# A DeltaNet recurrence and a SwiGLU feed-forward block: chunks of 64 tokens on 64x64 array tiles, with the triangular inverse moved from TensorE to VectorE

## The chip, the cores and the metric

The kernel runs on one core of one Trainium2 chip. The metric is the device time of the whole program in microseconds, as the median of a kernel's runs. Every kernel was run beside the kernel before on the same chip.

## The reference, cut to what matters

```python
# q, k, v: (4, 8, 768, 48) float32; beta: (4, 8, 768)
k_n = k / (np.linalg.norm(k, axis=-1, keepdims=True) + 1e-06)
for t in range(S):                                   # 768 tokens, one after the other
    kt, vt, bt = (k_n[:, :, t], v[:, :, t], beta[:, :, t, None])
    y[:, :, t] = np.einsum('bhd,bhde->bhe', q[:, :, t], state)
    v_old = np.einsum('bhde,bhd->bhe', state, kt)
    state = state + bt[:, :, :, None] * np.einsum('bhd,bhe->bhde', kt, vt - v_old)
# ... y becomes x: (4*768 tokens, 384)
g = x @ w_gate                                       # 384 x 1536
val = x @ w_val                                      # 384 x 1536
out = (g * (1.0 / (1.0 + np.exp(-g))) * val) @ w_out # 1536 x 384
```

The three weights arrive as float64, and the kernel has to turn them into fp32 itself.

## The kernel before

The tokens of one batch element are cut into chunks of C = 128. With S the state before a chunk and A, P the strictly lower triangles of two products of the chunk's rows, U = (I + A)^-1 (V - K S), Y = Q S + P U, and S grows by W^T U. A *unit* is one batch element and one chunk: 24 units. The inverse is built on TensorE by doubling: blocks of 2, 4, ... 128 rows, each level joined by two products and one transpose per head.

```python
        for s in levels:                             # 2, 4, 8, 16, 32
            p_a = ps_att([128, H, HC], "p_a")
            for h in range(H):
                nc.tensor.matmul(
                    p_a[:, h].rearrange("p (n r) -> p n r", r=s),
                    gq[:, h, 0],
                    even(x[:, h], s),
                )
            ax = work.tile([128, H, HC], FP32, name="ax")
            # ... VectorE: ax = p_a * sibling[s]
            yield
            p_d = ps_att([128, H, HC], "p_d")
            for h in range(H):
                nc.tensor.matmul(p_d[:, h], xt[:, h], ax[:, h])
            # ... VectorE: even blocks of x -= p_d
            yield
            transpose(xt, x)                         # 8 transposes (p_x) and 2 copies on ScalarE
            yield
        # ... the last level on halves of the rows; then U, Y, the new state, Y^T

    def ffn(c):                                      # a chunk of all four batch elements: 512 tokens
        for f in range(FT):
            # gate and val: KT = 3 matmuls each of 128 weight columns by 512 tokens
            # sil = Silu(p_gate) on ScalarE, h_f = sil * p_val on VectorE
        for b in range(B):
            # p_o: FT = 12 matmuls of 384 columns
    # emission: steps of two units in flight, steps of the FFN of an earlier chunk among them
```

Before the first FFN, VectorE converts the weights in 60 pieces with seven instructions each, one piece per round of the recurrence's steps.

## Time and profile before

| | before |
|---|---|
| time, median of 3 runs first, 4 runs beside the changed kernel | 1638.46 us, 1637.99 us |
| span of the profiled run | 1633.6 us |
| TensorE busy; records | 1519.6 us (93%); 9102 |
| VectorE, ScalarE, GpSimd busy | 30%, 17%, 15% |
| mean granted TensorE clock | 0.909 |

The profile counts every fp32 matmul as two records. "Busy" of TensorE is the time in which any record runs, so records of several array tiles that run side by side count once.

From the profile's page of the kernel before, the busy tenths of TensorE and VectorE in 40 equal slices (41 us each) and the granted clock in tenths; then the chain that ended last, by line:

```profile
PE   3985997999899999899899899899989999999999
...
DVE  7768764222122121222221212322122212122110
...
PEclk8875877999897799899899988789989989989999
...
PE p_a L347 15%; PE p_d L362 13%; PE p_gate L468 11%; PE p_val L468 10%; PE p_o L486 9%; PE p_x L325 8%; PE p_y L418 3%; POOL xt L328 3%; POOL xt L334 3%; PE p_u L400 3%; DVE gq L307 2%; DMA kpad<-in_k_dram 2%; PE p_d L384 2%; PE p_s L435 2%; POOL norm L267 1%
```

TensorE is nearly full from the third slice on. p_a, p_d and p_x, the three products of the inverse, are 15 + 13 + 8 + 2 = 38% of the chain, more than the whole FFN (11 + 10 + 9 = 30%). VectorE has room after the first six slices, where it converts weights.

### The profile page before, as it was taken

What the parts mean: (1) busy time and instruction counts of PE and PEld (TensorE: products, weight loads), DVE (VectorE), ACT (ScalarE), POOL (GpSimd) and SP (SyncE); (2) the same over time, 40 slices, a digit from 0 to 9 for tenths busy, and PEclk for the clock granted to TensorE, in tenths of its full rate; (3) what the DMA queues carried; (4) which work ended last, traced back from release to release, by engine and by line L of the source; (5) the groups of instructions that cost most, each with busy time, mean ns of one, the idle gap of its engine ahead of it and who ended that gap; (6) DMA issues with size and microseconds to landing.
All of it is one profiled execution on the core that took longest, in us unless ns stands there. A gap on an engine that the chain in (4) does not pass through costs nothing.

```text
span 1633.6 us, 21195 instructions
## 1 busy us (share of the span) xinstructions
PE 1519.6 (93%) x9102; PEld 1184.1 (72%) x9102; DVE 486.5 (30%) x1070; ACT 281.5 (17%) x531; POOL 247.2 (15%) x186
## 2 busy tenths in 40 slices
PE   3985997999899999899899899899989999999999
PEld 2984975776796777688577689577769767768745
DVE  7768764222122121222221212322122212122110
ACT  1121221111121121112112112112111212211210
POOL 6004016003103100401300500500120210020000
PEclk8875877999897799899899988789989989989999
DMA  8322201001001000101000100100100000000000
GB/s 182 91 75 52 59 11 29 1 10 26 10 16 20 1 1 11 29 11 28 2 1 11 30 10 11 20 1 1 25 10 11 15 1 1 6 11 10 1 0 20
DMA packets 90238, 35.09 MB, mean 21 GB/s; under 512 B 79360, under 2 KB 83968, under 8 KB 90144
## 3 DMA queue, kind: packets, MB, share of 16 engines
q1 hardware_dynamic: 86688, 29.01, 8.5%
q10 hardware_dynamic: 3456, 4.72, 0.8%
q8 instruction: 72, 1.18, 0.3%
q14 instruction: 22, 0.18, 0.0%
HBM read 29.00 MB, written 4.72 MB: 21 GB/s over the span
## 4 chain that ended last, share of the span: by engine, by line
PE 81%; POOL 10%; DVE 5%; DMA 2%; issue 1%; ACT 0%; POOLq 0%; SPq 0%
PE p_a L347 15%; PE p_d L362 13%; PE p_gate L468 11%; PE p_val L468 10%; PE p_o L486 9%; PE p_x L325 8%; PE p_y L418 3%; POOL xt L328 3%; POOL xt L334 3%; PE p_u L400 3%; DVE gq L307 2%; DMA kpad<-in_k_dram 2%; PE p_d L384 2%; PE p_s L435 2%; POOL norm L267 1%
## 5 line engine op out<-in xcount | busy, mean ns | idle before, releaser
L347 PEld LDWEIGHTS p_a<-x,gq 128*128 128x128 f32 x1920 | 261.0, 220 | 12.2 <-issue 9.6
L347 PE MATMUL p_a<-x,gq 128*128 128x64 f32 x1920 | 259.8, 301 | 0.0
L362 PEld LDWEIGHTS p_d<-ax,xt 128*128 128x128 f32 x1920 | 229.0, 197 | 13.4 <-issue 10.7
L362 PE MATMUL p_d<-ax,xt 128*128 128x64 f32 x1920 | 229.7, 280 | 0.0
L468 PE MATMUL p_gate<-x_ffn,wg_sb 128*128 128x512 f32 x432 | 212.6, 630 | 1.3 <-ACT x_ffn L458 1.1
L486 PE MATMUL p_o<-wo_sb,h_f 128*128 128x384 f32 x576 | 204.7, 504 | 0.0
L468 PE MATMUL p_val<-x_ffn,wv_sb 128*128 128x512 f32 x432 | 201.2, 602 | 0.0
L326 ACT COPY xt<-p_x 128x512 f32<-128x512 f32 x240 | 124.0, 595 | 419.8 <-PE p_x L325 419.8
L353 DVE TENSOR_TENSOR ax<-p_a,sibling 128x512 f32<-128x512 f32 x120 | 83.0, 691 | 370.2 <-PE p_a L347 369.8
L486 PEld LDWEIGHTS p_o<-wo_sb,h_f 128*128 128x128 f32 x576 | 109.1, 197 | 69.0 <-issue 10.6
L278 POOL TENSOR_TENSOR w<-kn,beta_t 128x512 f32<-128x512 f32 x24 | 25.4, 1058 | 782.2 <-PE p_s L435 781.8
L468 PEld LDWEIGHTS p_gate<-x_ffn,wg_sb 128*128 128x128 f32 x432 | 82.0, 202 | 84.1 <-issue 81.4
L364 DVE TENSOR_TENSOR x<-x,p_d 128x512 f32<-128x512 f32 x120 | 82.6, 688 | 192.6 <-PE p_d L362 192.6
L468 PEld LDWEIGHTS p_val<-x_ffn,wv_sb 128*128 128x128 f32 x432 | 78.4, 192 | 80.0 <-issue 79.7
L325 PEld LDWEIGHTS p_x<-ident,x 128*128 128x128 f32 x960 | 110.7, 146 | 17.6 <-issue 12.5
L325 PE MATMUL p_x<-ident,x 128*128 128x128 f32 x960 | 121.1, 279 | 0.0
L480 DVE TENSOR_TENSOR h_f<-sil,p_val 128x512 f32<-128x512 f32 x72 | 49.3, 685 | 237.1 <-PE p_val L468 237.0
L325 PE MATMUL p_x<-ident,xt 128*128 128x128 f32 x192 | 39.1, 370 | 76.0 <-POOL xt L334 76.0
L477 ACT ACTIVATE sil<-p_gate 128x512 f32<-128x512 f32 x72 | 43.0, 597 | 371.3 <-PE p_gate L468 371.3
L325 PEld LDWEIGHTS p_x<-ident,xt 128*128 128x128 f32 x192 | 31.0, 191 | 88.1 <-POOL xt L334 88.1
L328 POOL TENSOR_TENSOR xt<-gq,couple 128x1024 f32<-128x1024 f32 x24 | 56.9, 2372 | 165.3 <-DVE gq L307 165.3
L307 DVE SCALAR_TENSOR_TENSOR gq<-p_g,beta_t,mask_u 128x256 f32<-128x256 f32 x192 | 78.0, 474 | 12.8 <-PE p_g L304 12.8
(76 smaller groups left out, 1182.5 us busy)
## 6 DMA issues: line engine op xcount, KB each, us to landing
kpad<-in_k_dram SPq DMA_DIRECT2D x25, 192.0 KB, 4.4
qpad<-in_q_dram SPq DMA_DIRECT2D x25, 192.0 KB, 3.9
v_in<-in_v_dram SPq DMA_DIRECT2D x25, 192.0 KB, 2.8
staged<-in_moe_w_gate_dram SPq DMA_DIRECT2D x18, 256.0 KB, 3.7
staged<-in_moe_w_val_dram SPq DMA_DIRECT2D x18, 256.0 KB, 3.8
out_dram<-o_sb ACTq DMA_DIRECT2D x24, 192.0 KB, 1.9
staged<-in_moe_w_out_dram SPq DMA_DIRECT2D x12, 256.0 KB, 2.7
staged<-in_moe_w_out_dram SPq DMA_DIRECT2D x12, 128.0 KB, 2.0
```

The lines of the kernel that those rows point to most:

```text
L307: nc.vector.scalar_tensor_tensor(out=gq[:, h], in0=p_g[:, j], scalar=beta_t[:, c, b * H + h : b * H + h + 1], in1=mask_u[:, None, :].to_br ...
L325: nc.tensor.transpose(p_x[:, h], src[:, g + h], ident)
L326: nc.scalar.copy(dst[:, g : g + 4], p_x)
L328: nc.gpsimd.tensor_tensor(out=xt, in0=gq[:, :, 0], in1=couple[:, None, :].to_broadcast([128, H, 128]), op=ALU.mult,)
L334: nc.gpsimd.tensor_tensor(out=xt, in0=xt, in1=ident[:, None, :].to_broadcast([128, H, 128]), op=ALU.add,)
L347: nc.tensor.matmul(p_a[:, h].rearrange("p (n r) -> p n r", r=s), gq[:, h, 0], even(x[:, h], s),)
L353: nc.vector.tensor_tensor(out=ax, in0=p_a, in1=sibling[s][:, None, :].to_broadcast([128, H, HC]), op=ALU.mult,)
L362: nc.tensor.matmul(p_d[:, h], xt[:, h], ax[:, h])
L364: nc.vector.tensor_tensor(out=x_even, in0=x_even, in1=p_d.rearrange("p h j -> p (h j)").rearrange("p (n r) -> p n r", r=s), op=ALU.subtract,)
L468: nc.tensor.matmul(ps[name], w_sb[:, t, f * 128 : (f + 1) * 128], x[:, t], start=(t == 0), stop=(t == KT - 1),)
L480: nc.vector.tensor_tensor(out=h_f, in0=sil, in1=ps["p_val"], op=ALU.mult)
L486: nc.tensor.matmul(p_o, hs[f][:, b * C : (b + 1) * C], wo_sb[:, f], start=(f == 0), stop=(f == FT - 1),)
```

## The change

The intent is to take the inverse off TensorE, and to make the small products of the recurrence small on the array as well. Chunks become 64 tokens, so a unit is two batch elements of 64 tokens, and a head's product fits one 64x64 quarter of the array. Two chunks form a group: their 2 x 2 x 2 x 8 = 64 triangles of 64 rows give 128 diagonal blocks of 32x32, which go through DRAM so that each of VectorE's 128 partitions holds one block. There the inverse is made by substitution: 31 steps of a multiply and an add. It returns through DRAM, and two 32x32 products per head fill the off-diagonal block. The FFN runs per chunk of 256 tokens.

The core of the diff; "# ..." marks cuts:

```diff
-C = 128  # tokens of a chunk of the recurrence
+C = 64
+R = 32
# ... removed: masks of the levels, couple, the block mask of the state
-        for s in levels:
-            p_a = ps_att([128, H, HC], "p_a")
# ... removed: p_a, ax, p_d, x -= p_d, transposes p_x, per level; the last level
+    def prepare(g):
# ... norms and normalized k of two chunks, p_t: K^T and Q^T as before
+                p_g = ps_two([128, 2, NP, 2, C], "p_g")
+                for j in range(NP):
+                    for par, b in ((0, 0), (1, 1), (0, 1), (1, 0)):
+                        rows = slice(64 * par, 64 * par + 64)
+                        cols = slice(64 * b, 64 * b + 64)
+                        nc.tensor.matmul(
+                            p_g[cols, par, j],
+                            kq[n][rows, j, 0, cols],
+                            kq[n][rows, j, :, cols],
+                        )
# ... VectorE: a_sb and p_sb, masked
+        nc.sync.dma_start(out=a_d, in_=a_sb[g].rearrange("p u h i -> p (u h) i"))
# ... four reads of a_d into mb [128, 32, 32]: one block per partition
+        for j in range(R - 1):
+            m = R - 1 - j
# ...
+            nc.vector.tensor_tensor(
+                out=t_v,
+                in0=zb[:, 0 : j + 1, j : j + 1].to_broadcast([128, j + 1, m]),
+                in1=mb[:, j : j + 1, j + 1 : R].to_broadcast([128, j + 1, m]),
+                op=ALU.mult,
+            )
+            nc.vector.tensor_tensor(
+                out=zb[:, 0 : j + 1, j + 1 : R],
+                in0=zb[:, 0 : j + 1, j + 1 : R],
+                in1=t_v,
+                op=ALU.add,
+            )
# ... zb to z_d in DRAM, four reads into zt; then two 32x32 products (p_j) per head
+    ORDER = ((0, 0), (1, 1), (0, 1), (1, 0))
+    def advance(c):
# ... K S, Q S, U, the state and P U: 16 matmuls each, in this pattern
+                for j in range(NP):
+                    for par, b in ORDER:
+                        rows = slice(64 * b, 64 * b + 64)
+                        nc.tensor.matmul(
+                            p_s[64 * par : 64 * par + 64, b, j * D : (j + 1) * D],
+                            kn[rows, 2 * j + par],
+                            uu[rows, par, j],
# ...
     def ffn(c):
-        for f in range(FT):
+        for f in range(0, FT, 2):
# ... two weight blocks share a PSUM bank: [128, 2, 256]
+    some(prepare(0), everything)
+    some(advance(0), everything)
+    load_group(1)
+    behind = prepare(1)
+    some(behind, 10)
+    for c in range(NCH):
# ...
+        if c + 1 < NCH:
+            some(advance(c + 1), everything)
+        feed = ffn(c)
+        for n in range(FT // 2 + NB):
+            if c == 0:
+
+                some(converting, 2 * KT if n < FT // 2 else everything)
+            some(feed, 1)
+            some(behind, 2)
```

The order in which the program emits instructions is not quite the order on an engine: the build puts each engine's instructions in an order of its own that keeps to the dependences.

## The prediction

> **What bounds the kernel now.** I first read the busy shares on the page, then the share of the last chain by line, then the clock by stretch, and last the chain piece by piece to get the pace of each kind of matmul.
>
> ```profile
> PE 1519.6 (93%) x9102; PEld 1184.1 (72%) x9102; DVE 486.5 (30%) x1070; ACT 281.5 (17%) x531; POOL 247.2 (15%) x186
> ...
> PE 81%; POOL 10%; DVE 5%; DMA 2%; issue 1%; ACT 0%; POOLq 0%; SPq 0%
> ```
>
> TensorE is busy 93% and is 81% of the chain; nobody else is above 30%. So the question is how much TensorE time the change takes away, and whether waits then fill the space. A busy share says nothing about pace. That comes from the chain in order of time (start, length, line, records):
>
> ```profile
> 802.33 3.61 PE p_gate L468 x6
> 805.93 3.52 PE p_d L362 x32
> 809.45 2.63 PE p_val L468 x6
> 812.08 1.75 PE p_x L325 x16
> ...
> 816.41 3.52 PE p_a L347 x32
> ...
> 1599.41 30.97 PE p_o L486 x96
> ```
>
> Each fp32 matmul leaves two records (the code has 216 gate matmuls, the page 432; transposes leave one). The pace per record is 3.52/32 = 0.110 us for p_a and p_d (64 columns stream, 128 columns of weights), 1.75/16 = 0.109 for a transpose, 2.63/6 = 0.438 for 512 streamed columns (about 0.429 between steady starts), 30.97/96 = 0.323 for 384. The wide ones follow the streamed columns, 0.84 ns each; p_a and p_d do not, they follow the 128 weight columns. Two more lines, from the timeline of TensorE, show small array tiles:
>
> ```profile
> 917.68 2.10 PE L304 MATMUL p_g<-kq 64*128 64x256 f32 x16
> ...
> 1522.70 2.05 PE L384 MATMUL p_d<-xt,ax 64*64 64x64 f32 x32
> ```
>
> One tile of 64x64 alone steps at about (2.05-0.22)/31 = 0.059 us (0.22 is one record's length). The 64-row p_g, whose records alternate between the two row halves, steps at (2.10-0.38)/15 = 0.115, where 256 columns alone would cost 0.215: the two halves do run side by side.
>
> Full-clock sum: FFN 6 x (144 x 0.429 + 96 x 0.323) = 556 us. Recurrence: 3840 p_a/p_d x 0.110 = 422, 1152 p_x x 0.110 = 127, 768 p_u and p_y from u x 0.1125 = 86, 480 with the state x 0.1125 = 54, 384 p_g x 0.125 = 48, 264 other transposes x 0.11 = 29, 768 64x64 x 0.059 = 45: 811. Together 1367, and 1367/0.909 (mean granted clock) = 1504, against 1519.6 busy: the sum is sound.
>
> **What the Trainium skill says.** (1) "TensorE: Matmul & The Clock Gate", LDWEIGHTS: a weight load costs about P/1.2 ns, P its columns, whatever the rows: 107 ns for 128, 53 for 64. The trace agrees: 0.110 and 0.059. (2) "TensorEngine Tiling (Array Packing)", Key Properties: tiles work independently, weights and matmuls of different tiles in parallel, and a change of tiling mode drains the array. The trace shows two row tiles in parallel; four 64x64 tiles at once it does not show. (3) "VectorE: DVE Perf Modes", Mode 2x_2P: an fp32 tensor_tensor stays at one result a cycle. The trace agrees: 555 ns for 384 columns (L394), 691 for 512 (L353), so 1.06 ns a column plus about 150. (4) "DMA: Bandwidth & Descriptors", Anatomy of one DMA: about 2 us fixed (fitted there for the GpSimd path). The trace has 1.9 to 4.4 us to landing for 128 to 256 KB.
>
> **The change, part by part.** A unit is now two batches of 64 tokens; there are 24 again.
>
> *Removed:* all levels of p_a, p_d and p_x, 422+127+45 = 594 us of TensorE at full clock, with their copies on ACT (xt 124, x 27), DVE (ax 83, x 83) and POOL (xt 57+57).
>
> *Recurrence on small tiles, records per unit.* p_t 8 x 0.109 = 0.9 us. p_g 32 records, 128 streamed columns (0.107 alone), row halves alternating: two at once gives 0.054, 1.7 us. p_j 64 records of 32x32 on two row groups: estimate 0.025, 1.6. Advance: K S, Q S, U, state and P U are 16 matmuls each, 160 records, 64 weight columns and 48 streamed; 0.059 for a pair gives 0.03, 4.8. p_f 0.35. About 1.5 for changes of tile shape (my guess). Sum 10.9 us, 24 units = 260 us instead of 811.
>
> *FFN per 256 tokens.* 1728 records x 0.215 + 576 x 0.323 = 557 us: no change. Weight loads double, but 0.107 fits behind 0.215.
>
> So TensorE falls from 1367 to about 817 us at full clock.
>
> *Substitution, per group of two chunks (six groups).* 31 steps of two dependent DVE instructions; elements sum over j of (j+1)(31-j) = 5456, twice = 10912. RECIPROCAL after its input's instruction starts 35 ns after that one's end, so a dependent instruction costs about 150+35+1.04n: 62 x 0.185 + 10912 x 0.00104 = 11.5+11.3 = 23 us. Beside TensorE's 160 us per group this is small. Masks 8 x 0.62, norms 4, one multiply 1.1, transposes 1.4, copies 3: about 38 us of DVE per group.
>
> *Two round trips through DRAM per group.* 1 MB out (322 GB/s at best in this trace: 3.3 us, plus 2), then four reads of 1024 pieces; kpad, 1024 pieces too, takes 4.4 us to land and about 1.1 to issue: 4.4+3x1.1 = 7.7. About 13 us, and 11 for the way back. From the last mask to a usable zt, with the inverse's p_j: 13+23+11+10 = some 57 us of latency. Groups are prepared one to two chunks (46 us of FFN each) ahead, so in steady state most hides.
>
> **The start.** Here the change costs. Group 0 has nothing to hide behind: norms to about 13 us, four units at half clock to 35, then 57 or more and the advance: first FFN input near 115 to 130 us. And the weights' conversion is now emitted beside the first FFN chunk. By the page its DVE work is 155 us (L136 to L183 summed over both widths). DVE must do 155 + two groups x 38 + advances and h_f 8 = 239 us before that chunk is done, plus 15 of waits that conversion can't fill: about 254 us. TensorE runs perhaps 15 us ahead into chunk 1, so the rest starts as if at 240.
>
> **The rest, TensorE bound.** FFN 11 x 46.4 = 510. Prepare 16 units x 4.9 = 78; advance 20 units x 6 = 119 (drains shared out). Together 707 at full clock. The clock in the middle of the present run:
>
> ```profile
> 400.00:600.00 200.00, 188.33 (x1138) 151.71 (x1136) 46.23 (x81) 33.24 (x63) 32.60 (x20) 0.88 0.05 10
> 600.00:800.00 200.00, 187.66 (x1197) 146.76 (x1195) 48.61 (x90) 37.11 (x71) 41.22 (x28) 0.94 0.09 17
> 800.00:1000.00 200.00, 194.16 (x1203) 151.05 (x1203) 44.84 (x75) 33.94 (x65) 20.64 (x14) 0.96 0.05 11
> ```
>
> The eighth column is the clock. At 0.94, 707 becomes 752. Idle TensorE is 3 to 6% there; the new advance is a chain of short bursts, each waiting for a copy, and PSUM has two buffers where there were five, so I choose 10%: 835 us. 240+835 = 1075 us, a ratio of 0.66.
>
> **Rivals.** *No side-by-side tiles* (every 64x64 record 0.059): +4.6 advance, +1.7 p_g, +1 p_j per unit, about +150 us: 1225. For it: four tiles are not seen in the trace. Against: p_g shows two. *Round trips in the way:* if TensorE or the DVE's h_f stands behind each group's waiting instruction, up to 25 us for each of four groups, 1175. For it: engines take their instructions in order, and in the present trace TensorE stood 76 us for POOL's xt. Against: the conversion's instructions are interleaved across pieces on DVE, so the order is chosen with waits in mind. *DVE as the bound:* steady state needs 38 + 8 (h_f) + 6 of about 165 us per group, so no; at the start yes, and slower substitution steps or POOL in its way would add 30 to 60 us there. *Conversion done early*, in the idle start: 990 to 1010.
>
> **Range and chances.** The removed TensorE time is certain; pace of small tiles (+150), round trips (+100) and start (-60 to +60) are not, and the misses lean upward. I say 975 to 1220. Slower than 1606 would need 390 us of waits more than I count, after 140 allowed: 2%.
>
> **What would show it.** Right: TensorE busy near 900 us; advance records 0.03 us apart; gate and val 0.215; no L347, L362, L325 group; the first FFN chunk ending near 255 us with DVE full until then; clock at half before 100 us. Wrong: small-tile records 0.06 apart or more; TensorE below 80% after 260 us with DMA or DVE zb, mb as releaser; substitution above 30 us a group.

## The result, and the profile after

| | before | after |
|---|---|---|
| time, median of 4 runs each | 1637.99 us (1635.29 to 1639.12) | 952.32 us (951.05 to 954.01) |
| ratio | | 0.581, 95% interval 0.5795 to 0.5826 |
| TensorE busy; records | 1519.6 us; 9102 | 797.4 us; 8520 |
| VectorE busy | 486.5 us | 391.6 us |

A ratio is the mean time of one kernel's runs over the mean of the other's of the same rounds, so it is not quite the ratio of the medians. The result is 123 us below the prediction of 1075 and below its range.

From the page of the changed kernel: busy times, the same slices (24 us each now), and the chain by engine.

```profile
PE 797.4 (84%) x8520; PEld 609.6 (64%) x8520; DVE 391.6 (41%) x1079; ACT 132.7 (14%) x242; POOL 86.6 (9%) x84
...
PE   2400599466699998999989999989999999999998
...
DVE  4677228998823482222662122932124621101010
...
PE 65%; DVE 21%; DMA 5%; POOL 4%; issue 2%; SPq 1%; ACT 1%; ACTq 0%; POOLq 0%; DVEq 0%
```

There are two stages. For eleven slices, 262 us, TensorE has gaps (nine of the eleven tenths are 6 or less) and VectorE is often full; after that TensorE is full to the end. The end of the first FFN chunk (the copies of its two results start at 259.7 and 261.7 us) is the border. The rest, 689.9 us, is 72% of the span. The two stages in windows; the columns are the length, then busy time and instructions of TensorE, weight loads, VectorE, ScalarE and GpSimd, then the clock, the DMA share and GB/s:

```profile
60.00:90.00 30.00, 0.00 (x0) 0.00 (x0) 26.75 (x90) 0.00 (x0) 5.27 (x3) 1.00 0.06 25
90.00:120.00 30.00, 13.44 (x352) 12.03 (x352) 7.80 (x18) 3.37 (x9) 6.94 (x7) 1.00 0.22 39
...
160.00:200.00 40.00, 24.45 (x135) 16.86 (x133) 38.96 (x144) 1.79 (x3) 0.30 (x1) 0.74 0.26 76
200.00:260.00 60.00, 36.79 (x194) 21.43 (x194) 55.53 (x218) 2.58 (x6) 11.85 (x8) 0.91 0.42 111
```

```profile
262.00:400.00 138.00, 132.71 (x1709) 100.53 (x1712) 51.80 (x115) 24.16 (x48) 14.22 (x12) 0.98 0.21 46
400.00:600.00 200.00, 195.01 (x2158) 150.53 (x2149) 68.21 (x149) 33.31 (x59) 14.22 (x12) 0.99 0.22 48
600.00:800.00 200.00, 194.65 (x2260) 149.08 (x2260) 75.42 (x174) 32.74 (x64) 13.06 (x10) 0.98 0.14 31
800.00:950.00 150.00, 146.96 (x893) 114.97 (x892) 14.05 (x21) 17.23 (x32) 0.00 (x0) 1.00 0.03 8
```

In the start, VectorE alone works from 60 to 90 us (substitution of group 0 and some conversion), then idles, then is full from 160 us on with the rest of the conversion. In the rest, which I call the second stage, TensorE is busy 669.3 of 688 us, so idle 2.7%, at a clock of 0.98 to 1.00 (0.987 weighted by length).

Why is it so full? The timeline of TensorE in a piece of this stage (start, length, line, what, records):

```profile
319.74 2.10 PE L528 MATMUL p_o<-wo_sb,h_f 128*128 128x384 f32 x6
321.76 1.15 PE L428 MATMUL p_y<-state,kq 64*64 64x48 f32 x64
322.84 1.13 PE L511 MATMUL p_gate<-x_ffn,wg_sb 128*128 128x256 f32 x4
323.90 1.14 PE L447 MATMUL p_u<-r,zt 64*64 64x48 f32 x32
324.97 1.13 PE L511 MATMUL p_gate<-x_ffn,wg_sb 128*128 128x256 f32 x4
326.03 0.68 PE L463 MATMUL p_s<-uu,kn 64*64 64x48 f32 x32
326.53 1.10 PE L481 MATMUL p_y<-uu,p_sb 64*64 64x48 f32 x32
```

Three things are to be read here. The 64 records of K S and Q S step at (1.15 - 0.22)/63 = 0.015 us, 0.22 being one record's length. Between K S and U, and between U and the state, where a subtraction on VectorE or a copy on ScalarE must come first, stand four records of gate, about 1.1 us of other work: no idle time is noted. The program emits advance(c + 1) as a whole before ffn(c), so it is the build's order that put them there. And a change between 128x128 and 64x64 tiles is not free. On the way in, six p_o records should take 6 x 0.323 = 1.94 us from 319.74 to 321.68, and the small ones start at 321.76. Then four gate records should take 4 x 0.2155 = 0.86 us, and from 322.84 to 323.90 they take 1.06. Decoded from the trace, in the second stage: the last gate or val record before a small burst takes 0.309 us instead of 0.216, the first one after it 0.320, and the last small record mostly 0.12 to 0.15 until the FFN's next start, instead of about 0.02. Together that is about 0.33 us there and back, 112 times: some 36 us. What in the change takes this time no run here separates.

What is left of waiting of TensorE, summed over the run, by what it waited for (us in total, times, longest):

```profile
PE p_j L392 <- DMA zt<-z_d: 55.8, 2, 54.2
PE p_o L528 <- DVE wo_sb L222: 18.3, 9, 3.7
...
PE p_gate L511 <- DVE h_f L522: 14.1, 4, 4.5
```

The 54.2 us is group 0, at the start, with nothing to hide behind. Conversion is the start, too: wo_sb, and further down the same view wv_sb (10.8 us) and wg_sb (8.7), 37.8 us together. Of these lines only the one for h_f is of steady state: 13.3 of its 14.1 us, in three places. One of them, in the chain in order of time:

```profile
350.94 2.94 POOL norm L284
353.90 1.44 DVE norm L285
...
357.38 2.87 POOL norm L284
360.27 0.90 DVE norm L285
361.36 0.64 DVE h_f L522
362.04 3.35 PE p_gate L511 x7
```

GpSimd's power for the norm takes 2.9 us, VectorE stands waiting for it, and the FFN's h_f stands behind it on VectorE. The gate matmul does not read h_f; by the code it needs one of the FFN's three PSUM buffers, and p_val's comes free when h_f has read it.

### The profile page after: what moved, and what is told of

The parts are those of the page before. It is cut to its first block, busy times and chain, and to the rows that moved or that the text cites. A ratio compares the mean times of both kernels' runs of the same rounds, so it can differ in the third digit from the quotient of the medians.

```text
span 951.5 us, 19339 instructions
## 1 busy us (share of the span) xinstructions
PE 797.4 (84%) x8520; PEld 609.6 (64%) x8520; DVE 391.6 (41%) x1079; ACT 132.7 (14%) x242; POOL 86.6 (9%) x84
## 4 chain that ended last, share of the span: by engine, by line
PE 65%; DVE 21%; DMA 5%; POOL 4%; issue 2%; SPq 1%; ACT 1%; ACTq 0%; POOLq 0%; DVEq 0%
PE p_o L528 19%; PE p_gate L511 16%; PE p_val L511 15%; DVE tmp L360 5%; DVE zb L366 5%; PE p_g L317 3%; POOL norm L284 2%; PE p_u L447 2%; PE p_j L392 2%; PE p_y L481 2%; PE p_j L405 2%; PE p_y L428 2%; PE p_t L305 1%; DMA staged<-in_moe_w_val_dram 1%; DVE power L214 1%
## 5 line engine op out<-in xcount | busy, mean ns | idle before, releaser
L511 PE MATMUL p_gate<-x_ffn,wg_sb 128*128 128x256 f32 x864 | 225.2, 405 | 23.0 <-DVE h_f L522 14.1
L511 PE MATMUL p_val<-x_ffn,wv_sb 128*128 128x256 f32 x864 | 209.0, 386 | 10.8 <-DVE wv_sb L222 10.8
L511 PEld LDWEIGHTS p_gate<-x_ffn,wg_sb 128*128 128x128 f32 x864 | 165.9, 200 | 53.4 <-DVE h_f L522 15.4
L511 PEld LDWEIGHTS p_val<-x_ffn,wv_sb 128*128 128x128 f32 x864 | 163.0, 193 | 36.2 <-DVE wv_sb L222 7.4
L366 DVE TENSOR_TENSOR zb<-zb,tmp 128x31 f32<-128x31 f32 (+15 forms) x186 | 67.5, 363 | 4.1
L360 DVE TENSOR_TENSOR tmp<-zb,mb 128x31 f32<-128x31 f32 (+15 forms) x186 | 63.6, 342 | 4.4
L317 PE MATMUL p_g<-kq 64*64 64x128 f32 x768 | 30.0, 300 | 12.0 <-DVE p_sb L323 8.2
L305 PE MATMUL p_t<-ident,kn 128*128 128x128 f32 x96 | 26.7, 309 | 15.0 <-POOL kn L290 15.0
L317 PEld LDWEIGHTS p_g<-kq 64*64 64x64 f32 x768 | 23.6, 147 | 20.2 <-issue 10.9
L284 POOL TENSOR_TENSOR norm<-norm,half 128x16 f32<-128x16 f32 x12 | 35.3, 2938 | 8.7 <-DVE norm L280 8.7
L307 ACT COPY kq<-p_t 128x1024 f32<-128x1024 f32 x24 | 24.3, 1013 | 67.0 <-PE p_t L306 67.0
```

What stands on the lines that cost most here:

```text
L284: nc.gpsimd.tensor_tensor(out=norm_f, in0=norm_f, in1=half, op=ALU.pow)
L305: nc.tensor.transpose(p_t[:, j, 0], kn[:, pair], ident)
L307: nc.scalar.copy(kq[n], p_t)
L317: nc.tensor.matmul(p_g[cols, par, j], kq[n][rows, j, 0, cols], kq[n][rows, j, :, cols],)
L360: nc.vector.tensor_tensor(out=t_v, in0=zb[:, 0 : j + 1, j : j + 1].to_broadcast([128, j + 1, m]), in1=mb[:, j : j + 1, j + 1 : R].to_broad ...
L366: nc.vector.tensor_tensor(out=zb[:, 0 : j + 1, j + 1 : R], in0=zb[:, 0 : j + 1, j + 1 : R], in1=t_v, op=ALU.add,)
```

## The experiments

Thirteen kernels ran, three rounds each. Times are medians, with the lowest and highest run; "first gate" and "end of the first FFN chunk" are start times in the trace. They follow here by the question they answer.

### What the levels cost: b_no_levels

The kernel before without p_a, p_d, p_x and their copies. Its output is wrong, which doesn't matter for the time.

```diff
-        transpose(x, xt)
-        yield
-        for s in levels:
# ... all of the levels removed; the last level as well
```

> The kernel before with the inverse cut down to its first level (no p_x, p_a, p_d; a wrong result on purpose), everything else as it was, 128-token chunks and full array. If it is the inverse leaving TensorE that gives nearly all of the gain, 594 us at full clock go, about 640 at the clock granted: 950 to 1020 us, as fast as the changed kernel. If the short dependent steps then bound it (two units in flight), above 1150; if the small tiles matter as much as the inverse, clearly above 1020 as well, with TensorE busy 90%.

Measured: 1006.08 us (1004.69 to 1007.03), ratio 0.6143 [0.613, 0.6155]; relative error 0.834.

```profile
PE 865.1 (86%) x3342; PEld 538.7 (54%) x3342; DVE 304.8 (30%) x806; ACT 116.2 (12%) x219; POOL 247.3 (25%) x186
```

Taking the levels off TensorE is worth 1636 - 1006 = 630 us by itself, against the 594 us at full clock (653 at the old clock of 0.909) that the prediction worked out. Of the 686 us that the change brought, all the rest (small tiles gained, the start and the inverse's new home lost) nets about 54 us, if the parts are taken to add up: the run without levels has waits of its own (TensorE is 86% busy), and it took the levels' copies off the other engines as well.

### Whether small tiles run side by side: e_one_tile and e_two_tiles

Both keep the instructions and change only the order of the matmuls: e_one_tile puts the ones of one array tile after each other, e_two_tiles alternates between two.

```diff
-                for j in range(NP):
-                    for par, b in ORDER:
+                for par, b in ORDER:
+                    for j in range(NP):
# e_two_tiles: for pair in (((0,0),(1,1)), ((0,1),(1,0))): for j: for par, b in pair
```

> The changed kernel with its loops turned round, so that four matmuls in a row use the same array tile (same arithmetic, same result). If the small matmuls are cheap because different tiles run at the same time, their records go from 0.016 to 0.033 us apart to about 0.058 (0.107 in p_g), some 8 us more per unit; 16 units of p_g and 20 of the advance come after the start, so 150 us more: about 1100 us. If TensorE has room for it beside other waits, under 40 us more: below 990.

> The changed kernel with the tiles visited in two pairs, first the pair on the diagonal four times, then the other pair, so that at most two tiles can run at once, which is what my prediction counted. If four at once is what made the unit 7.2 us instead of the predicted 10.9, then K S and Q S go back from 0.017 to 0.03 us a record, p_s from 0.016 to 0.03 and p_g from 0.032 to 0.054, 2 us a unit, 35 to 40 us in all: about 990 us. If two at once was already all there was: 952.

Measured: e_one_tile 1048.88 us (1047.85 to 1049.32), ratio 0.6404 [0.6391, 0.6416]; e_two_tiles 966.49 us (965.34 to 968.22), ratio 0.5902 [0.589, 0.5915]; both correct. The same K S and Q S burst as above, in the timeline of e_one_tile and then of e_two_tiles:

```profile
349.96 2.58 PE L428 MATMUL p_y<-state,kq 64*64 64x48 f32 x64
```

```profile
324.40 1.51 PE L435 MATMUL p_y<-state,kq 64*64 64x48 f32 x64
```

That is (2.58 - 0.22)/63 = 0.037 and (1.51 - 0.22)/63 = 0.020 us a record, against 0.015 with four tiles in turn. Decoded from the changed kernel's trace, the records of K S come in fours 0.007 us apart, one four every 0.058 us, and those of U in twos, one pair every 0.058 us. So four tiles do run side by side, each at nearly the 0.059 of one tile alone. U and P U come in pairs because, by the code, their operands and results lie in the same half of the rows: they can use only two of the four tiles in any order, and step at 0.029 us in the changed kernel and at 0.026 to 0.030 in e_two_tiles. The order of the loops alone is worth 97 us. Both runs missed their figures. e_one_tile was to take 1100 us, but the records of one tile did not all step at 0.059: between steps of 0.058 stand pairs of 0.041 and 0.018, so runs on two tiles overlap where they meet, and the mean is 0.037. e_two_tiles was to take about 990 us and lost only 14 us: its pairs overlap too where they meet (steps of 0.007, 0.004 and 0.007 stand side by side), so its 0.020 is not the pace of two tiles alone, which is the 0.029 of U.

### Where the waits of the recurrence went: e_rec_only and e_no_fill

e_rec_only drops the FFN and the weights and writes y to the output. Its output is wrong, which doesn't matter for the time.

```diff
-        feed = ffn(c)
# ... weights, staging, conversion and ffn() removed
+            for b in range(2):
+                nc.scalar.dma_start(
+                    out=out_v[2 * bp + b, c * C : (c + 1) * C],
+                    in_=y[64 * b : 64 * b + 64].rearrange("p h d -> p (h d)"),
+                )
```

> The changed kernel's recurrence alone: no weights, no conversion, no FFN; y is stored as the output (a wrong result on purpose). TensorE's work in it is some 173 us. If the recurrence is full of waits that only the FFN's matmuls fill in the whole kernel, it takes 450 to 600 us alone, so that FFN (557 us) plus recurrence is well over 952. If its waits are few by themselves (which would also explain that the 10% I allowed did not come), it takes 250 to 350 us.

Measured: 601.68 us (600.7 to 606.97), ratio 0.3673 [0.3664, 0.3682], 2 us above the expected 450 to 600; relative error 74.4. TensorE is busy 246.8 us of it (41%). The largest wait of TensorE:

```profile
PE p_j L299 <- DMA zt<-z_d: 231.8, 12, 48.5
```

The recurrence alone needs 602 us, the FFN by its records 557 us; one after the other would be 1159 us, and the changed kernel takes 952. So some 206 us of the two lie beside each other; fewer, if the recurrence alone, whose clock was 0.652 in the profiled run, is counted at the clock that it has beside the FFN. What binds it alone are the round trips through DRAM, 48.5 us at the longest, which the changed kernel's steady state hides. But the prediction had hidden these too; what it had not hidden were the short waits inside the advance. For these, e_no_fill: two ties that change no value make the advance of a chunk and the FFN beside it take turns.

```diff
     def ffn(c):
+        if c + 1 < NCH:
+            for t in range(KT):
+                nc.vector.scalar_tensor_tensor(
+                    out=x[:, t, 0:1],
+                    in0=xts[c + 1][:, KT - 1, TOK - 1 : TOK],
+                    scalar=0.0,
+                    in1=x[:, t, 0:1],
+                    op0=ALU.mult,
+                    op1=ALU.add,
+                )
# ... and after o_sb, likewise: state += 0 * o_sb, four parts of the state
```

> The changed kernel with two ties that change no value (an operand multiplied by zero is added): the recurrence's advance of a group waits for the end of the feed-forward part before it, and the feed-forward part waits for the end of the next group's advance, so that the two can no longer lie beside each other on TensorE; only the prepare steps of the next group still can. Theory A (the advance has long waits, as the prediction thought, and the feed-forward records fill them, which is why the predicted 10% of idle time and its lower clock did not come): +70 to +110 us on 952, so 1025 to 1065 us, with a lower clock in the rest. Theory B (the advance's waits are short by themselves, and nothing has to fill them): under +30 us, so below 985 us. The result is to be correct.

Measured: 1038.35 us (1035.68 to 1045.12), ratio 0.6327 [0.6298, 0.6356], correct. The windows of its second stage, which begins at 278.5 us and takes 764.9 us:

```profile
400.00:600.00 200.00, 181.07 (x2150) 138.15 (x2151) 61.20 (x164) 30.52 (x59) 16.40 (x15) 0.95 0.19 40
600.00:800.00 200.00, 186.89 (x1850) 145.19 (x1848) 61.86 (x159) 29.27 (x51) 13.03 (x10) 0.96 0.17 37
800.00:1000.00 200.00, 185.81 (x1728) 146.81 (x1721) 46.23 (x132) 25.74 (x51) 0.00 (x0) 0.96 0.06 13
```

And some of TensorE's waits:

```profile
PE p_u L447 <- DVE r L437: 15.5, 16, 1.7
...
PE p_s L463 <- ACT uu L456: 12.9, 22, 0.6
...
PE p_f L496 <- ACT y L490: 6.6, 14, 0.6
```

The kernel is 86 us longer, inside theory A's range. In the profiled runs (1043.4 against 951.5 us) the second stage took 75 us more (764.9 against 689.9) and the start 17 us. From 260 to 1000 us TensorE idles 64.5 of 740 us, 8.7%, and the clock is 0.940 weighted by length, where the changed kernel has 2.7% and 0.987. (From 278.5 us to the end it is 63 of 765 us, 8.2%, against 20 of 690, so 43 of the 75 us are idle time; the others are for the most part records that step more slowly.) The waits of the advance, p_u for r and p_s for uu and p_f for y, are there in most of the 24 units, up to 1.7 us long; in the changed kernel the sums for them are 2.8, 1.2 and 1.8 us. So it is the FFN's records that fill them. One reservation: the ties add a handover of their own each way (7.1 us before x_ffn in eleven places, 8.1 us before the state in ten), so not all of the 86 us is filling lost.

### What substitution costs: e_double_subst

Each multiply runs twice, with the same values. Each add runs twice as well, but the second one's result goes into the scratch tile, where nothing reads it.

```diff
# each step: the multiply into t_v, the same multiply again, the add into zb, and then:
+            nc.vector.tensor_tensor(
+                out=t_v,
+                in0=zb[:, 0 : j + 1, j + 1 : R],
+                in1=t_v,
+                op=ALU.add,
+            )
```

> The changed kernel with each multiply and each add of the substitution done twice, the second time into the scratch tile (correct result): 124 DVE instructions a group instead of 62, some 24 us more. If the substitution is hidden beside the FFN in steady state, as I predicted, only the first two groups cost, one in the first group's chain and one where DVE is full: 35 to 50 us more, 985 to 1000 us, and the time from 262 us (then some 305) to the end stays near 690. If it stands in the way in each group, six times 24: 1075 to 1095.

Measured: 982.48 us (980.39 to 984.06), ratio 0.5997 [0.5977, 0.6017], correct, a little below the expected 985 to 1000. VectorE is busy 511.6 us instead of 391.6. The end of the first FFN chunk moves from 259.7 to 296.5 us, while the second stage is 680.4 us and thus no longer than before. (It is even 9.5 us shorter; the waits for h_f there fell from 13.3 to 0.7 us, though nothing was done about them. So some 10 us can come and go with a shifted order alone.) So substitution costs time for the first groups only; in steady state doubling its 22 us of work per group is hidden. This is the case of an engine that is off the path.

### What binds the start: e_conv_early, e_conv_mid, e_one_op, e_conv3, e_mid_conv3

e_conv_early emits the whole conversion right after prepare(0); e_conv_mid after advance(0) and ten steps of prepare(1). e_one_op replaces the seven conversion instructions by one copy (wrong). e_conv3 uses three: it shifts and masks bits rather than computing, cuts off the low bits instead of rounding, and leaves out the clamps for numbers beyond fp32's range. e_mid_conv3 is e_conv_mid and e_conv3 together.

```diff
# e_conv_early and e_conv_mid
+    some(converting, everything)
-            if c == 0:
-                some(converting, 2 * KT if n < FT // 2 else everything)
# e_conv3, instead of seven instructions
+            # bits = (high << 3) & 0x3FFFFFF8
+            # bits = (low >> 29) | bits
+            # dst  = (high & 0xC0000000) | bits
# e_one_op
+            nc.vector.tensor_copy(dst[:, t, f0 : f0 + m], high.bitcast(FP32))
```

> The changed kernel with the whole conversion of the weights emitted right after the first group's preparation instead of among the first FFN chunk (correct result). In the trace the conversion stops at 85 us and begins again at 144 us: its staging buffers are of one tag with h_f and are handed out in order of emission, so piece 14 waits for the first h_f. If the start is bound by DVE's 155 us of conversion plus what else DVE does, and the idle 60 us of DVE before 144 can be used, the first FFN chunk ends 40 to 60 us sooner: 895 to 915 us. If the start is bound by the latency of the first group (first FFN input at 122 us) and TensorE catches up anyway, under 15 us: above 937.

> As the run with the early conversion, but with the conversion emitted after the first group's advance and the second group's masks, so that it only takes DVE time those leave (correct result). The early one ended its first FFN chunk 38 us sooner but began it 36 us later (166 us against 130), because conversion stood before the first advance. If that delay is what ate its gain, the first FFN input comes at 130 to 140 us, the chunk ends by 215 and the whole takes 900 to 915 us. If DVE's sum of work binds the start whatever the order, 925 to 940.

> The changed kernel with one DVE copy a piece instead of seven instructions (weights wrong on purpose), 420 to 60 DVE instructions and some 140 us of DVE less, order of emission as it was. By the sum of the prediction the start then is bound by the first group's latency (122 us to the first FFN input) and the FFN's own 46 us: the first chunk ends near 180 us instead of 262, 70 to 80 us less: 870 to 885 us. If the conversion does not bind, above 930.

> The changed kernel with three DVE instructions a piece (shift and mask, or with the shifted low word, or with sign and top exponent bit) instead of seven; the order of emission as it was. The weights are cut off instead of rounded, which should pass the comparison. DVE's conversion falls from some 150 to 50 us. By the one-copy run (902 us with 16 us of conversion) the start is then bound half by DVE and half by staging buffers that h_f holds: 905 to 920 us.

> Both: three instructions a piece, emitted before the first FFN chunk. If DVE's work and the shared staging buffers together are what holds the start, neither is left, the first FFN input comes at 120 to 130 us, the chunk ends by 190 and the whole takes 865 to 885 us, below the one-copy run's 902, which still had the shared buffers. If only DVE's work counts, as the one-copy run or more: 900 to 910.

| kernel | time, us (range) | ratio [95%] | first gate | end of first FFN chunk (first of its two copies) | last conversion |
|---|---|---|---|---|---|
| after | 952.32 (951.05 to 954.01) | 0.581 [0.5795, 0.5826] | 129.8 | 259.7 | 258.4 |
| e_conv_early | 931.93 (929.43 to 932.72) | 0.5686 [0.5668, 0.5705] | 165.9 | 221.6 | 162.4 |
| e_conv_mid | 931.02 (930.47 to 934.15) | 0.5682 [0.566, 0.5704] | 141.3 | 220.6 | 185.7 |
| e_one_op (wrong, error 29036) | 901.59 (900.05 to 903.24) | 0.5504 [0.5483, 0.5526] | 117.2 | 204.8 | 202.6 |
| e_conv3 | 920.85 (919.37 to 921.93) | 0.5615 [0.5595, 0.5636] | 121.9 | 227.5 | 226.2 |
| e_mid_conv3 | 899.64 (896.64 to 900.82) | 0.5484 [0.5462, 0.5506] | 135.1 | 190.8 | 132.7 |

In the changed kernel the last conversion and the end of the first FFN chunk are 1.3 us apart. That alone does not show who waits for whom (in e_one_op, with cheap copies, they are 2.2 us apart too); but VectorE is full from 160 us on, TensorE's waits for converted weights are 37.8 us, and fewer conversion instructions end the chunk sooner. e_conv_early fills VectorE's empty time, as the windows of it show beside those of the changed kernel above:

```profile
60.00:90.00 30.00, 0.00 (x0) 0.00 (x0) 30.00 (x116) 0.00 (x0) 0.36 (x1) 0.50 0.45 113
90.00:120.00 30.00, 1.73 (x46) 1.46 (x48) 24.30 (x76) 0.36 (x1) 11.64 (x8) 0.50 0.40 110
```

The first FFN chunk's first copy then comes 38 us sooner and its second one, from which I count the second stage, 32 us, but the program ends only 20 us sooner (24 in the profiled runs): the first gate comes 36 us later, since conversion now stands in front of group 0 on VectorE, and the second stage takes 698 us instead of 690. That this is because TensorE has less done ahead is my reading. It fell between its two expected ranges: moving the work helps, by half of what I expected. e_conv_mid let the first gate come 25 us sooner than e_conv_early and was no faster, as its second theory said: the order no longer matters much once VectorE is full. Less work on VectorE does: e_conv3 alone brought 31 us (it missed its range of 905 to 920 by 0.85 us), and both together 53 us, near the sum (21 + 31) and 0.4 us below the upper of its two expected ranges. e_one_op brought 51 us, less than its first theory expected: with the order unchanged, its last copies come at 202.6 us although they are cheap.

Why does conversion pause between 85 and 144 us in the changed kernel? The loads of the fifteenth piece and later ones were issued from 141.5 us on, the moment at which the first h_f was written. Pieces and h_f share eight buffers in the order of emission, and the loads also stand in one queue with other loads that wait. I did not separate these two: no kernel with staging buffers of its own was run.

### The norm's wait: e_norm_pool and e_all

e_norm_pool moves the norm's add and reciprocal to GpSimd, so that VectorE's h_f no longer stands behind an instruction that waits for GpSimd. e_all has this, the three-instruction conversion and its earlier place.

```diff
-            nc.vector.tensor_scalar_add(norm_f, norm_f, 1e-6)
-            nc.vector.reciprocal(norm_f, norm_f)
+            nc.gpsimd.tensor_scalar_add(norm_f, norm_f, 1e-6)
+            nc.gpsimd.tensor_tensor(out=norm_f, in0=norm_f, in1=minus, op=ALU.pow)
```

> The changed kernel with the last two steps of the norm (add, reciprocal as a power of -1) on POOL instead of DVE (correct within fp32 rounding). In the steady part TensorE stands three times some 4.5 us for h_f, which on DVE is queued behind the norm's add, which waits for POOL's power. If that queueing is the cause, these three waits go and with them the half clock after them, against some 3 us more in the first group's chain: 935 to 945 us. If h_f was late for another reason (the reads through DRAM), no change: 950 to 955, waits of 4.5 us still there.

> Both, and the norm's last two steps on POOL. Its effect alone was 5 us (three waits of 4.5 us for h_f went, two of 4.3 us for zt came). Here 0 to 8 us below the run with both: 860 to 880 us. If POOL's longer chain delays the first group more than it saves, 2 to 5 us above it.

Measured: e_norm_pool 946.92 us (944.54 to 949.63), ratio 0.5781 [0.576, 0.5802], correct. The 13.3 us of waits for h_f are gone, the second stage is 681.1 us instead of 689.9 (e_double_subst, which leaves the norm alone, lost these waits as well, so their going is no proof by itself; the chain shown above is what ties them to the norm), but the wait for the inverse's way back from DRAM, absent from the changed kernel's steady state, takes part of it:

```profile
PE p_j L394 <- DMA zt<-z_d: 66.0, 4, 56.4
```

Four waits where there were two, and about 8.5 us in the second stage: GpSimd's chain per group is longer now (group 0's wait for kn grew from 15.0 to 24.4 us), so the group is ready later. So the gain was 5.4 us and not 13, between the two expected ranges. e_all took 891.99 us (889.79 to 892.5), ratio 0.5441 [0.5418, 0.5464], correct. That is 6.3% less than the changed kernel (by the medians) and the best of all, though it missed its expected 860 to 880: its second stage is 700.7 us. Whoever takes it over must accept a conversion that truncates and is meant for weights within fp32's normal range.

## Why the prediction was wrong

The direction was right and the size was not: 1075 us with a range from 975, against 952. The prediction's last sum was 240 + 835. Measured, it is 262 + 690, and its terms differ as follows (record times are start to next start, decoded from the trace between 262 us and the end).

| term | predicted | measured | difference |
|---|---|---|---|
| start, "as if at" | 240 | 262 | +22 |
| FFN records of the rest | 510 | 504 (1551 x 0.2155 + 527 x 0.3226) | -6 |
| recurrence records of the rest, without changes of tile shape | 197 - 27 = 170 | 123 | -47 |
| changes of tile shape of the rest | 16 x 0.7 + 20 x 0.8 = 27 | 36 | +9 |
| waits and clock of the rest | 835 - 707 = 128 | 690 - 504 - 123 - 36 = 27 | -101 |
| sum | 1075 | 952 | -123 |

The 27 us of changes are what the predicted 4.9 and 5.95 us a unit hold beyond their records. The last but one row can be checked: 18.7 us of idle time and 669 x (1 - 0.987) = 8.7 us for the clock are 27 us.

**The removed work** was right: TensorE lost what the levels took, and b_no_levels gives 630 us for it.

**The step that failed first** is "the new advance is a chain of short bursts, each waiting for a copy, and PSUM has two buffers where there were five, so I choose 10%", with the clock of 0.94 taken over from the kernel before. The mechanism it names exists, but not in this kernel: e_no_fill, where the FFN cannot stand in the gaps, idles 8.7% at a clock of 0.940, near the 10% and 0.94 that I chose (about 15 us of its idle time are the ties' own). The changed kernel idles 2.7% at 0.987, because FFN records, often four, stand between one burst and the next. So 27 us came where I had allowed 128. Of a wait for the recurrence's PSUM buffers nothing is to be seen in the second stage; the only PSUM wait there is the FFN's, 13.3 us for h_f. I had seen that orders are chosen with waits in mind (on VectorE, for the conversion), and used it only against a rival. The lower clock was then counted on top of idle time that did not come.

**The step that failed second** is the pace of small tiles: "0.059 for a pair gives 0.03, 4.8". It was right for U and P U, which by the code can use only two tiles (0.029 us a record). It was wrong for K S, Q S, the state and p_g, which use four: 0.015 instead of 0.03, and 0.027 instead of 0.054 for p_g; p_j steps at 0.017 instead of 0.025. The advance's 160 records take 3.3 us instead of 4.8. The trace before showed two tiles at most, so "a pair" was the most I let stand. **The guess** of 1.5 us a unit for changes of tile shape was about right, a little low: some six times there and back a unit are about 2 us. A unit is then 6.4 us of records and 2.0 of changes, 8.4 instead of 10.9.

**The start** was right in its result (first FFN input predicted 115 to 130 us, seen 129.8; end of the first FFN chunk predicted 254, seen 260) but partly by luck. I counted 239 us of VectorE work before that point, nearly all the time there is. The durations of its instructions up to 262 us do sum to 228 us, but they lie over each other (a 0.42 us instruction is followed by the start of the next after 0.33 us where the next does not depend on it), so VectorE was busy only 182 of the first 260 us. The kernel before has it already: its conversion's 155 us are a sum of durations, and VectorE is busy 126 us with them. The pause of some 60 us in the conversion, which I had not foreseen, made up for it. TensorE was not 15 us ahead at the end of this stage, but about 7 (33 of the next chunk's gate and val records). In the table the 15 were taken off the start (254 became 240), while the 7 stand in the FFN row, where 33 records fewer are counted; the end itself came 8 us later than predicted.

**Substitution** was right: 63.6 + 67.5 = 131 us of VectorE for six groups are 22 us each, predicted 23. **The round trips** were hidden in steady state, as the prediction held against its own rival. Group 0 took longer than the 57 us predicted: from its last mask at 43.3 us to the end of the last p_j at 113.9 us are 71 us: about 10 for the way out (13 predicted), 31 for the mask product and the substitution (23; conversion instructions stand in between), 12 until the way back is usable (11), and 17 for p_j (10), whose bursts each wait about 1 us for a copy.

**The rivals.** *No side-by-side tiles* would have been 150 us dearer by the prediction; it is false, and even one tile at a time costs only 97. *Conversion done early* did not happen in the changed kernel, and made by hand it was worth 20 us, not the 65 to 85 that the rival's 990 to 1010 meant. *Round trips in the way* did not come true; *DVE as the bound* did at the start only, as said.

**The signs named in advance.** TensorE busy near 900 us: it was 797. Advance records 0.03 us apart: 0.029 for U and P U, 0.015 for the others. No group of L347, L362 and L325: right. Gate and val at 0.215: right. VectorE full to the end of the first chunk: wrong, as above. None of the three signs of being wrong appeared; all three looked for a kernel slower than predicted. The clock at half before 100 us: the clock column says 1.00 up to 160 us, but the records say half. Two equal bursts of p_g in the timeline of the changed kernel:

```profile
30.66 1.99 PE L317 MATMUL p_g<-kq 64*64 64x128 f32 x32 [8.20 <-DVE p_sb L323]
...
131.28 1.10 PE L317 MATMUL p_g<-kq 64*64 64x128 f32 x32
```

The early burst takes almost twice as long, and transposes step at 0.21 us there and at 0.11 from 129 us on. In this profile the clock column missed the slow time at the start; e_conv_early's, above, has 0.50 there. So the run's mean clock of 0.975 is too high (the other three runs have 0.915 to 0.929), and here the pace of the records is the safer witness.

## What to carry to other kernels

A chain of short bursts on the busiest engine costs its waits only if nothing independent can stand between the bursts: look for such work in the same instruction stream before allowing idle time, and do not lower the clock for idle time that is filled. Matmuls that fit a quarter of the array are worth ordering so that neighbours fall on different tiles: here the loop order alone was worth 97 us. Each change of tile shape has a price (about 0.33 us there and back here), so bursts that are cut up to fill gaps should not be cut finer than the gaps need. When steady state is full, the next gain lies in the start; here less of one engine's work (the weights' conversion) brought 31 us, its order 21, and both together 53.

## What the Trainium skill lacked or had wrong

- "TensorEngine Tiling (Array Packing)", Key Properties: it says that a change of tiling mode drains the array, and gives no time. Here a change from 128x128 to 64x64 or 32x32 tiles and back took about 0.33 us in all (0.309 instead of 0.216 for the FFN record before, 0.320 for the one after, 0.149 instead of about 0.02 for the last small record), 36 us in the second stage. How much of that is a drain no run shows.
- "TensorE: Matmul & The Clock Gate", the section "Wait — 56ns, not 53.3ns?": it gives about 25 ns as the least distance from start to start, however small the matmul. With four 64x64 tiles in turn the trace has 15 ns on average and 7 ns within a group of four. So that sentence is too broad across tiles: the same page's part on packing, "Measured speedup vs the span model", counts about 4 ns for each further tile.
- No page gives the cost of a power on GpSimd: 128x16 elements took 2938 ns (128x8 took 1648 ns in the kernel before), more than the multiply of 128x384 elements beside it (843 ns), and steady state waited for it.
